# Moving 45 on-chip buffers to other addresses: attention into a SoLU feed-forward layer on one core

## The chip, the core and the metric

The program runs on one core of a Trainium2 chip. The metric is the device time of one execution in microseconds (us). A kernel is timed in several runs and its median is given; beside that, one further execution was profiled, and all durations of single instructions below come from that one. The engines are named as in the profile: PE (matmuls) and PEld (its weight loads), DVE, ACT and POOL (elementwise work), SP (the queue that issues all DMA transfers).

## What is computed

The reference is an attention between 512 tokens and 32 states in each of 8 batches and 8 heads, in both directions, and behind it a feed-forward layer with a softmax-weighted activation and a layer norm:

```python
# x: (8, 8, 512, 64), state: (8, 8, 32, 64), scale = 1 / 8
a = softmax(scale * x @ state.T)              # tokens read the states
xread = a @ state
a2 = softmax(scale * state @ x.T)             # states read the tokens
sread = a2 @ x
x = concat([xread, sread], axis=2)            # as rows: 8 * (512 + 32) = 4352 x 512

h = x @ w_in                                  # 4352 x 1024
sm = softmax(h)
solu = h * sm
mu, var = solu.mean(-1), solu.var(-1)
ln = (solu - mu) / sqrt(var + 1e-6) * g_ln
out = ln @ w_out                              # 4352 x 512
```

Inputs and output are float32.

## The kernel before, in words

**Tiling.** The 4352 rows are 34 tiles `t` of 128: 32 tiles hold the token rows (four for each batch), and the last two hold the state rows of all batches. A tile goes through five steps. `H`: PE multiplies into `h`, a 128x1024 PSUM tile (line 472). `C`: DVE takes the row maximum (479), ACT the exponential `e` (482), DVE the product `u` (485), ACT or DVE subtracts the mean in place (490, 492), ACT squares and sums (497), and POOL makes the row factor (499 to 502). `D`: DVE transposes 32x32 blocks into `ub` (509), a DMA writes it to a DRAM buffer (326), and another reads it back as `back` with the blocks in their final places (331). `T`: `back` is split into a rounded part `uh` (ACT or DVE, 141 and 143) and the rest `ul` (POOL or DVE, 146). `O`: PE multiplies them with the split weights `wohi` and `wolo` (546), ACT or DVE scales the result into `osb` (553, 555), and a DMA writes that out (559). In a matmul here the 128x128 piece of `uh` or `ul` is loaded as weights, and 512 columns of `wohi` or `wolo` stream past it.

**Before the tiles** the weights are loaded as `raw`, turned into float32 (`wf`) and split; for each batch the states are multiplied with `w_in` (`swf`, `vt`), the scores are made and go through both softmaxes (`e2`, `a`, `aT`, `ath`, `atl`).

**What sets the order.** Each engine's instructions stand in the order of a fixed list, `ORDER`, and nothing is rescheduled. Each step is a generator, and each token of the list runs one step to its next `yield`.

**What sets the addresses.** SBUF tiles come from pools, and a pool lays its tiles down one behind the other in the order of their first use. There are 45 common blocks of 4096 bytes in each partition. Which block a tile takes is fixed too: the string `PLACES["k4"]` has one character for each tile in order of use, and each character is one of the 45 places, so that a block holds one tile after the other. Before the change the blocks come from the pool `work`, the same one that gives the small tiles: `r` (2048 bytes), `s2` (2048), `sc` (16), `m1` and `z1` (up to 128 each), `sm` (32), `sr` (512) and `osb` (2048). A small tile that is first used between two blocks therefore stands between them and pushes the later blocks on. The pool `const`, laid down first in both kernels, ends at byte 21216, which is 5 x 4096 + 736.

Added up, the 45 blocks begin at these positions (start address modulo 4096):

| position before | blocks | pushed there by |
|---|---|---|
| 736 | 1 (place 0, at 21216) | nothing; it is the first |
| 2784 | 22 | three `r` tiles (6144 bytes), further on also the two `s2` tiles (4096) |
| 2848 | 2 | the two `sc` tiles (32 each) |
| 2976 | 15 | `m1` (128) |
| 3104 | 5 | `z1` (128) |

Place 0 holds, one after the other, `raw0`, `vt7_0`, `ub8`, `u10`, `uh10`, `atl4`, `a7`, `ub28` and `ub31` (the number is that of the weight piece, the batch or the tile). The eight operands that stream in the `O` step stay at one place each from the splitting of the weights on: three of the four `wohi` blocks begin at 2976 and one at 2784; three of the four `wolo` blocks begin at 2784 and one at 3104.

Of the kernel before, what the change touches and what calls it, by code (L numbers as in the profile page):

```python
# [8 lines left out]
F32 = mybir.dt.float32  # L9
# [7 lines left out]
B, H, S, NS, D = 8, 8, 512, 32, 64  # L17
DM, DF = 512, 1024
P = 128
NP = H // 2  # L20
NT = S // P
NJ = H * NS // P
# [61 lines left out]
    k4='0123456789ABCDEFGHIJKLMNOPQRSTUVWXYZabcdefghi0148BAFEKLQPNTOefcdMR6USgJVcTdLNOaZgI6APCWY7BDcKXbLhgiG'  # L84
# [20 lines left out]
def attention_then_solu_ffn(ctx, tc, xT, xn, stB, w_in, w_out, g, out):  # L105
    nc = tc.nc
    const = ctx.enter_context(tc.tile_pool(name="const", bufs=1))
    work = ctx.enter_context(tc.tile_pool(name="work", bufs=1))
    dram = ctx.enter_context(tc.tile_pool(name="dram", bufs=B + NTILES, space=bass.MemoryType.DRAM))
    kept = ctx.enter_context(tc.tile_pool(name="kept", bufs=4, space=bass.MemoryType.DRAM))  # L110
# [7 lines left out]
    def place(tag):  # L118
        return f"{tag}_{next(places[tag])}"

    def sbuf(tag, shape, dtype, name):
        if tag in places:
            return work.tile(shape, dtype, tag=place(tag), name=name, bufs=1)
        return work.tile(shape, dtype, tag=tag, name=name, bufs=SLOTS[tag])

    def block(shape, dtype, name):
        return sbuf("k4", [P, *shape], dtype, name)

    def bank(shape, name):
        return ps_t.tile([P, *shape], F32, tag=place("t"), name=name, bufs=1)  # L130
# [41 lines left out]
    def load_st(k):  # L172

        st[k] = block([2 * NP * 2, 2, NS], F32, f"st{k}")
        nc.sync.dma_start(st[k].rearrange("p (k c s) h n -> p k c s (h n)", k=2, c=NP), stB[:, k:k + 2])
        yield
# [24 lines left out]
    def load_x(b, j):  # L201
        x_of[b, j] = block([2, S], F32, f"xT{b}_{j}")
        nc.sync.dma_start(x_of[b, j], xT[b][:, 2 * j:2 * j + 2])
        yield

    def load_xn(b, i):

        xn_of[b, i] = block([2, H * D], F32, f"xn{b}_{i}")
        nc.sync.dma_start(xn_of[b, i], xn[b].rearrange("(c f) p h -> (f p) c h", c=4)[:, 2 * i:2 * i + 2])
        yield  # L210
# [113 lines left out]
    def to_dram(x, name):  # L324
        d = dram.tile([P * DF], F32, tag="d", name=name)
        nc.sync.dma_start(d.rearrange("(p f) -> p f", p=P), x)
        return d

    def from_dram(out, d):

        nc.sync.dma_start(out.rearrange("p (q c) -> p q c", q=4), d.rearrange("(q p c) -> p q c", q=4, p=P))
# [10 lines left out]
    def softmax_tokens(b):  # L342

        sc = sbuf("sc", [P, 4], F32, f"sc{b}")
        for j in range(NJ):
            ps = scores[b][j]
            nm, z = sc[:, j:j + 1], sc[:, 2 + j:3 + j]
            nc.vector.tensor_reduce(nm, ps, AX.X, ALU.max, negate=True)
            yield
            nc.gpsimd.tensor_scalar_mul(nm, nm, float(D) ** -0.5)  # L350
            yield
            if j == 0:
                e2 = block([NJ, S], F32, f"e2T{b}")
            nc.scalar.activation(e2[:, j, :], ps, AF.Exp, bias=nm, scale=float(D) ** -0.5, accum_out=z)
            yield
        z = zs[b] = sc[:, 2:4]
        nc.vector.tensor_scalar_add(z, z, 1e-9)
        nc.vector.reciprocal(z, z)
        yield
        blocks = block([NJ * S], F32, f"e2b{b}")  # L360

        nc.vector.transpose(blocks.rearrange("x (p j c) -> x j p c", p=4, j=NJ),
                            e2.rearrange("x j (p c) -> x j p c", p=4))
        yield
        d = to_dram(blocks, f"e2d{b}")
        yield
        e2s[b] = block([NJ * S], F32, f"e2_{b}")
        from_dram(e2s[b], d)
        yield
# [219 lines left out]
    for b in range(B):  # L589
        for i in range(2):  # L590
            step(f"LT{b}{i}", load_x, b, i)
            step(f"Ln{b}{i}", load_xn, b, i)
            step(f"V{b}{i}", state_w_in, b, i)
        step(f"S{b}", score, b)
        step(f"E{b}", softmax_tokens, b)
        if b in OPT["ah"]:
            for part in range(2):
                step(f"Ah{b}{part}", softmax_states, b, part, 2)
        else:
            step(f"A{b}", softmax_states, b)  # L600
        step(f"R{b}", read_tokens, b)
        for j in range(NJ):
            step(f"Y{b}{j}", keep_state_w_in, b, j)
            step(f"Z{b}{j}", load_state_w_in, b, j)
            step(f"P{b}{j}", split_state_w_in, b, j)
# [49 lines left out]
```

## Time and profile before

| what | us |
|---|---|
| median of 3 runs | 372.08 |
| lowest and highest of them | 370.94, 375.21 |
| the profiled execution | 372.63 |
| its span, from the first instruction to the last | 370.8 |
| its mean granted TensorE clock | 0.978 |

The profile is read as follows. A group row gives line, engine, operation, the tiles written and read, the sizes and the count, then the busy time in us, the mean of one in ns, and the idle time of the engine ahead of these instructions with what ended it. A tile row gives for all instructions that touch a tile the least, the median and the greatest duration in ns. The chain of waits follows the work that ended last back from the end, and gives shares of the span. Buffer numbers are left out of names (`ub` stands for all 34 of them), so a single tile is found by its time.

### The profile page before, as it was taken

To read this page: it belongs to the slowest core of one execution; us is meant where nothing else is said; L and a number is where in the kernel's file an instruction comes from. 1 tells how busy PE (TensorE), PEld (TensorE's weight loads), DVE (VectorE), ACT (ScalarE), POOL (GpSimd) and SP (SyncE) were. 2 spreads that over 40 slices of the span, in tenths; PEclk is the share of its full clock that TensorE was granted. 3 is DMA by queue.
4 is the path that set the end of the run, shared out by engine and by line. 5 is a ranking of instruction groups with operands and counts; after the bars stand their busy time and mean duration, and the time that the engine had idled before them with its cause. 6 is when DMAs were issued, how large, how long until landed. Compare 5 with 4: busy or idle time off the path is not lost.

```text
span 370.8 us, 6200 instructions
## 1 busy us (share of the span) xinstructions
PE 348.9 (94%) x2274; PEld 255.3 (69%) x2274; DVE 282.4 (76%) x393; ACT 216.3 (58%) x350; POOL 190.5 (51%) x245
## 2 busy tenths in 40 slices
PE   5498999989999999999999999999999999999990
PEld 4163334468777877778877777887888887888890
DVE  4679999979897978969979998969579577665400
ACT  3277998876768863847755656372474645424230
POOL 2131365565678662527776247376866616702540
PEclk9599999999999999999999999999999999999996
DMA  7996999999879999486895796846662454245412
GB/s 254 396 401 226 348 307 337 345 351 319 315 241 324 343 354 319 166 277 203 266 358 203 244 369 232 276 158 248 217 229 95 151 189 170 85 177 183 150 63 56
DMA packets 47051, 92.16 MB, mean 249 GB/s; under 512 B 4141, under 2 KB 25901, under 8 KB 47021
## 3 DMA queue, kind: packets, MB, share of 16 engines
q1 hardware_dynamic: 47020, 91.77, 70.7%
q8 instruction: 18, 0.29, 0.3%
q14 instruction: 13, 0.10, 0.1%
HBM read 54.53 MB, written 37.22 MB: 247 GB/s over the span
## 4 chain that ended last, share of the span: by engine, by line
PE 70%; DMA 13%; DVE 9%; ACT 3%; issue 2%; SPq 1%; POOL 1%; DVEq 0%; POOLq 0%
PE o L546 40%; PE h L472 22%; DMA ut<-ub 4%; DMA back<-ut 3%; DMA st<-stB_dram 3%; PE swps L198 2%; DMA xT<-xT_dram 2%; PE sps L198 2%; PE srps L420 2%; PE swph L198 2%; DVE ub L509 1%; DMA e<-e2d 1%; DVE sm L479 1%; DVE u L485 1%; ACT u L490 1%
## 5 line engine op out<-in xcount | busy, mean ns | idle before, releaser
L146 POOL TENSOR_TENSOR ul<-back,uh 128x512 fp32r<-128x512 f32 x46 | 61.2, 1335 | 49.5 <-DVE uh L143 23.8
L546 PE MATMUL o<-wolo,uh 128*128 128x512 f32 (+1 forms) x264 | 72.2, 388 | 0.0
L546 PE MATMUL o<-wohi,ul 128*128 128x512 f32 (+1 forms) x264 | 72.2, 387 | 0.0
L546 PE MATMUL o<-wohi,uh 128*128 128x512 f32 (+1 forms) x264 | 71.5, 389 | 0.4 <-ACT uh L141 0.2
L482 ACT ACTIVATE e<-h,sm 128x1024 f32<-128x1024 f32 x34 | 37.8, 1113 | 40.0 <-DVE sm L479 36.7
L546 PEld LDWEIGHTS o<-wohi,uh 128*128 128x128 f32 x264 | 48.3, 188 | 12.9 <-ACT uh L141 0.9
L485 DVE SCALAR_TENSOR_TENSOR u<-h,e 128x1024 f32<-128x1024 f32 x34 | 41.4, 1217 | 20.6 <-ACT e L482 20.2
L546 PEld LDWEIGHTS o<-wohi,ul 128*128 128x128 f32 x264 | 48.7, 188 | 11.6 <-issue 0.8
L546 PEld LDWEIGHTS o<-wolo,uh 128*128 128x128 f32 x264 | 48.3, 188 | 12.2 <-issue 1.7
L479 DVE TENSOR_REDUCE sm<-h 128x1 f32<-128x1024 f32 x34 | 41.3, 1213 | 15.4 <-PE h L472 8.4
L509 DVE STREAM_TRANSPOSE ub<-u 128x1024 f32<-128x1024 f32 x34 | 42.0, 1237 | 5.2 <-ACT u L490 4.6
L141 ACT ACTIVATE uh<-back 128x512 fp32r<-128x512 f32 (+1 forms) x46 | 28.2, 624 | 26.3 <-DMA back<-ut 26.3
L497 ACT ACTIVATE e<-u 128x1024 f32<-128x1024 f32 x34 | 35.8, 1053 | 5.6 <-DVE u L492 5.3
L553 ACT ACTIVATE osb<-o,sm 128x512 f32<-128x512 f32 (+1 forms) x29 | 19.3, 668 | 27.8 <-PE o L546 9.7
L472 PE MATMUL h<-swh,ath 128*128 128x512 f32 x112 | 35.3, 401 | 0.0
L472 PE MATMUL h<-swl,ath 128*128 128x512 f32 x112 | 35.0, 394 | 0.0
L472 PE MATMUL h<-swh,atl 128*128 128x512 f32 x112 | 34.9, 394 | 0.0
L490 ACT ACTIVATE u<-u,sm 128x1024 f32<-128x1024 f32 x20 | 23.0, 1150 | 14.4 <-DVE u L485 14.4
L146 POOL TENSOR_TENSOR swl<-swf,swh 128x1024 fp32r<-128x1024 f32 x11 | 26.6, 2418 | 3.3 <-ACT swh L141 2.1
L248 POOL TENSOR_TENSOR wf<-wf,r 128x512 uint32<-128x512 uint32 x9 | 11.8, 1311 | 27.7 <-DVE wf L245 11.3
L472 PEld LDWEIGHTS h<-swh,ath 128*128 128x128 f32 x112 | 20.6, 188 | 6.2 <-issue 1.2
L472 PEld LDWEIGHTS h<-swh,atl 128*128 128x128 f32 x112 | 21.0, 188 | 4.9
(87 smaller groups left out, 531.6 us busy)
## 6 DMA issues: line engine op xcount, KB each, us to landing
ut<-ub SPq DMA_DIRECT2D x34, 512.0 KB, 3.5
back<-ut SPq DMA_DIRECT2D x34, 512.0 KB, 4.6
out_dram<-osb SPq DMA_DIRECT2D x33, 256.0 KB, 3.5
xT<-xT_dram SPq DMA_DIRECT2D x16, 512.0 KB, 6.9
xn<-xn_dram SPq DMA_DIRECT2D x16, 512.0 KB, 5.7
kept<-vt SPq DMA_DIRECT2D x12, 512.0 KB, 6.3
swf<-kept SPq DMA_DIRECT2D x12, 512.0 KB, 5.7
raw<-w_in_dram SPq DMA_DIRECT2D x8, 512.0 KB, 8.8
```

Source lines behind the costliest of these rows:

```text
L141: nc.scalar.activation(out, src, AF.Copy)
L146: engine(k).tensor_tensor(out=out, in0=a, in1=hi.bitcast(F32), op=ALU.subtract)
L198: nc.tensor.matmul(banks[j][at:at + NS, :], state_of(b, head), moving(head // 2)[h * D:(h + 1) * D], start=True, stop=True)
L472: nc.tensor.matmul(ph[t][:, cols], left[l][:, p, tok], weights[:, cols], start=(p, l, r) == (0, 0, 0), stop=(p, l, r) == (parts - 1, *kind ...
L479: nc.vector.tensor_reduce(nm, ph[t], AX.X, ALU.max, negate=True)
L482: nc.scalar.activation(e, ph[t], AF.Exp, bias=nm, accum_out=z)
L485: nc.vector.scalar_tensor_tensor(out=u, in0=ph[t], scalar=1.0, in1=e, op0=ALU.mult, op1=ALU.mult, accum_out=su)
L490: nc.scalar.activation(u, u, AF.Identity, bias=su, scale=-float(DF))
L497: nc.scalar.activation(e, u, AF.Square, scale=float(DF) ** -0.5, accum_out=ss)
L509: nc.vector.transpose(ub, us[t][0])
L546: nc.tensor.matmul(po, ut[t][l][:, f, :], w[NP + f // 2][:, f % 2, cols], start=(hf, l, w is wohi, q) == (0, 0, True, 0), stop=(hf, l, q) ...
L553: nc.scalar.activation(o[:, cols], po, AF.Copy, scale=us[t][1])
```

## The change

The 45 blocks get a pool of their own, `blocks`, which is opened between `const` and `work`. Only one helper, `block()`, gives out tiles of this kind; it now asks that pool, with the same tag for each place. A local variable that had the pool's new name is renamed.

```diff
@@ attention_then_solu_ffn
     const = ctx.enter_context(tc.tile_pool(name="const", bufs=1))
+    blocks = ctx.enter_context(tc.tile_pool(name="blocks", bufs=1))
     work = ctx.enter_context(tc.tile_pool(name="work", bufs=1))
...
     def block(shape, dtype, name):
-        return sbuf("k4", [P, *shape], dtype, name)
+        return blocks.tile([P, *shape], dtype, tag=place("k4"), name=name, bufs=1)
...
-        blocks = block([NJ * S], F32, f"e2b{b}")
-
-        nc.vector.transpose(blocks.rearrange("x (p j c) -> x j p c", p=4, j=NJ),
+        turned = block([NJ * S], F32, f"e2b{b}")
+
+        nc.vector.transpose(turned.rearrange("x (p j c) -> x j p c", p=4, j=NJ),
                             e2.rearrange("x j (p c) -> x j p c", p=4))
         yield
-        d = to_dram(blocks, f"e2d{b}")
+        d = to_dram(turned, f"e2d{b}")
```

The blocks now stand one behind the other from byte 21216 on, and as each is 4096 bytes long, all 45 begin at position 736 modulo 4096. Place 0 stays where it was; the 22 blocks at 2784 move by 2048 bytes modulo 4096, the others by 2112, 2240 and 2368. The small tiles come behind the blocks, from byte 205536 on. 45 times 4096 is a whole multiple of 4096, so each small tile keeps the position modulo 4096 that it had (`r` at 736, 2784 and 736, `s2` at 2784 and 736, `osb` at 3744 and 1696), and `sm`, `sr` and `osb`, which were last in the pool before too, even keep their addresses.

On each engine and in SP's queue the same instructions stand in the same order, with the same sizes and the same semaphore waits. Which tile shares a block with which is the same too. Only addresses differ.

## The prediction

> **What bounds the kernel now.** I read the page's first part and the chain of waits first, to see which engine the end hangs on, and then busy time by stage. The first row gives busy time and share of the span for each engine, the next two the chain's shares by engine and by line, the table the same stretch by stretch.
>
> ```profile
> span 370.8 us, 6200 instructions
> PE 348.9 (94%) x2274; PEld 255.3 (69%) x2274; DVE 282.4 (76%) x393; ACT 216.3 (58%) x350; POOL 190.5 (51%) x245
> ...
> PE 70%; DMA 13%; DVE 9%; ACT 3%; issue 2%; SPq 1%; POOL 1%; DVEq 0%; POOLq 0%
> PE o L546 40%; PE h L472 22%; DMA ut<-ub 4%; DMA back<-ut 3%; DMA st<-stB_dram 3%; PE swps L198 2%; DMA xT<-xT_dram 2%; PE sps L198 2%; PE srps L420 2%; PE swph L198 2%; DVE ub L509 1%; DMA e<-e2d 1%; DVE sm L479 1%; DVE u L485 1%; ACT u L490 1%
> ```
>
> ```profile
> core 0: us, PE busy (x) PEld busy (x) DVE busy (x) ACT busy (x) POOL busy (x), PEclk, DMA share, GB/s
> 0.00:80.00 80.00, 68.07 (x522) 33.55 (x522) 64.81 (x104) 55.74 (x95) 30.70 (x44) 0.94 0.91 326
> 80.00:180.00 100.00, 99.33 (x659) 76.25 (x660) 85.77 (x112) 67.92 (x108) 62.17 (x75) 1.00 0.83 287
> 180.00:280.00 100.00, 99.17 (x711) 77.96 (x710) 83.73 (x115) 59.16 (x94) 60.55 (x76) 1.00 0.73 255
> 280.00:345.00 65.00, 65.00 (x289) 52.52 (x288) 44.99 (x59) 27.84 (x46) 28.11 (x37) 1.00 0.43 150
> 345.00:371.00 26.00, 17.38 (x99) 14.99 (x97) 3.08 (x6) 5.61 (x10) 8.97 (x16) 0.88 0.25 82
> ```
>
> From 80 to 345 us PE is busy in 263.5 of 265 us. The time there is the number of matmuls times the pace of one. Before 80 us transfers take part (DMA share 0.91), and behind 345 us the last tile's chain runs out. So a new address can reach the end in three ways: by PE's pace, by transfers (13% of the chain, 48.2 us), or by DVE, ACT and POOL where the chain passes through them (9%, 3% and 1%).
>
> **The change, part by part.** It adds no instruction, removes none and moves none; no wait is new, and no DMA passes another. The only cost it can have is a duration that depends on where a tile begins. The trace of before already holds tiles at five positions, and place 0 stands at 736, where all blocks go. So I look for that dependence in it, engine by engine.
>
> PE first, as it carries 70% of the chain. The chain's longest unbroken stretches give the pace; its columns are the start, the length in us, and the piece of work with its number of matmuls. Then the group rows by form for streamed operands, and the spread of the weight loads in the tile view.
>
> ```profile
> 168.56 9.25 PE o L546 x40
> ...
> 280.73 9.73 PE o L546 x42
> ...
> 312.79 8.78 PE o L546 x38
> ```
>
> ```profile
> L546 PE MATMUL o<-wolo,uh 128*128 128x512 f32 x248 | 69.9, 395 | 0.0
> L546 PE MATMUL o<-wohi,ul 128*128 128x512 f32 x248 | 69.8, 394 | 0.0
> L546 PE MATMUL o<-wohi,uh 128*128 128x512 f32 x248 | 69.1, 396 | 0.4 <-ACT uh L141 0.2
> ```
>
> ```profile
> L546 PEld LDWEIGHTS o<-wohi,uh x264: 186/188/192, 81.6 to 361.0; 128*128 128x128 f32 x132
> L546 PEld LDWEIGHTS o<-wolo,uh x264: 186/188/192, 82.4 to 361.5; 128*128 128x128 f32 x132
> L546 PEld LDWEIGHTS o<-wohi,ul x264: 186/188/192, 83.3 to 362.0; 128*128 128x128 f32 x132
> ```
>
> The pace is 9250/40 = 231.3, 9730/42 = 231.7 and 8780/38 = 231.1 ns. `wohi` streams mostly from 2976, `wolo` mostly from 2784 (three of four blocks each), and their means are 394 to 396 ns: 1 ns between the kinds, and no more between the two rows of `wohi` itself. The weights `uh` and `ul` come from all five positions, and 264 loads lie within 186 to 192 ns. I take 0 for PE. The bound is 1 ns on each 512-column matmul of this kind. Those are 3 x 248 here, 3 x 112 in `H` and 3 x 16 for the state rows (the rows of `h` read the same way), 1128 in all: 1.1 us either way.
>
> DVE, ACT and POOL next. The first two rows cover all 34 tiles at every position (least/median/greatest ns). The timeline rows behind them (start and duration in us) are instructions on place 0, already at 736: `u10` written at 131.99 and read at 137.40, changed in place at 133.42, `ub28` written at 301.58, and `atl4` written at 177.37.
>
> ```profile
> L485 DVE SCALAR_TENSOR_TENSOR u<-h,e x34: 1164/1224/1227, 44.3 to 343.1; 128x1024 f32<-128x1024 f32 x34
> ...
> L509 DVE STREAM_TRANSPOSE ub<-u x34: 1186/1245/1247, 46.7 to 345.2; 128x1024 f32<-128x1024 f32 x34
> ...
> L490 ACT ACTIVATE u<-u,sm x20: 1133/1152/1156, 45.6 to 306.5; 128x1024 f32<-128x1024 f32 x20
> ```
>
> ```profile
> 131.99 1.23 DVE L485 SCALAR_TENSOR_TENSOR u<-h,e 128x1024 f32<-128x1024 f32 x1 [1.27 <-ACT e L482]
> ...
> 137.40 1.24 DVE L509 STREAM_TRANSPOSE ub<-u 128x1024 f32<-128x1024 f32 x1
> ```
>
> ```profile
> 133.42 1.14 ACT L490 ACTIVATE u<-u,sm 128x1024 f32<-128x1024 f32 x1
> ```
>
> ```profile
> 301.58 1.25 DVE L509 STREAM_TRANSPOSE ub<-u 128x1024 f32<-128x1024 f32 x1
> ```
>
> ```profile
> 177.37 2.41 POOL L146 TENSOR_TENSOR atl<-aT,ath 128x1024 fp32r<-128x1024 f32 x1
> ```
>
> ```profile
> L146 POOL TENSOR_TENSOR atl<-aT,ath 128x1024 fp32r<-128x1024 f32 x4 | 9.7, 2426 | 6.4 <-ACT ath L141 5.4 <-DVE ath L143 1.0
> ```
>
> At the new position each takes its group's median to 0.01 us (1.23 against 1.224, 1.24 and 1.25 against 1.245, 1.14 against 1.152, 2.41 against a mean of 2.426). I take 0. The bound is 0.01 of about 1.2 us, some 0.8%, on the 13% of the chain that lies on these engines (48.2 us): 0.4 us either way. Elsewhere PE's work covers it; PE's own operands would come late only if that cover of POOL and DVE ran out.
>
> Transfers are last, and the least sure, because their time to landing depends above all on what else is in flight. The tile view of `ub` gives over all (least/median/greatest):
>
> ```profile
> DMA to landing us min/median/max: 2.6/3.5/6.6
> ```
>
> I compare single transfers at quiet moments: at 302.9 us (`ub28`, from place 0 at 736), at 259.5 (`ub23`, from 2976) and at 154.4 (`ub11`, from 2784). The three answers, one for each moment, follow in that order.
>
> ```profile
> L326 SPq DMA_DIRECT2D ut<-ub x1: 319/319/319, 302.9 to 302.9; - x1
> ...
> DMA to landing us min/median/max: 2.6/2.6/2.6
> ```
>
> ```profile
> L326 SPq DMA_DIRECT2D ut<-ub x1: 332/332/332, 259.5 to 259.5; - x1
> ...
> DMA to landing us min/median/max: 2.6/2.6/2.6
> ```
>
> ```profile
> L326 SPq DMA_DIRECT2D ut<-ub x1: 319/319/319, 154.4 to 154.4; - x1
> ...
> DMA to landing us min/median/max: 2.6/2.6/2.6
> ```
>
> All three land after 2.6 us. I take 0; the row's last digit leaves 0.05 in 2.6, or 2%, and on the 48.2 us of the chain that is 1.0 us either way.
>
> [...] The quiet transfers from 736, 2784 and 2976 show no difference in their tenth of a us; none from 2848 or 3104 was as quiet.
>
> The sum: 372.63 us of the profiled execution (370.8 span, 1.8 around it) plus 0, between 2.5 less and 2.5 more if all bounds fell on one side. That execution lies 0.55 above the median of the three runs, so against the median the forecast is 372.08 plus 0, rounded to 372.0.
>
> **The rivals.** First, slower: every tile now begins at the same position, and each long transfer's row crosses a multiple of 4096 after 3360 bytes, where before it was 992 to 1312 for all but place 0. If transfers between blocks and DRAM took longer for it, the place to feel it is the bounce `ut<-ub`, `back<-ut` in the chain and the loads before 80 us, where DMA is busy 91% of the time. At 10% more the chain's 48.2 us give 4.8 us, 376.9 in all; it decides from 7.7% on (3.7 of 48.2). For it speaks only that one transfer in three of these is not seen at a quiet moment; against it, that `ub28` with the new crossing landed in 2.6 us like the others, and that every row crosses one such multiple before as well as after.
>
> Second, faster: PE streams more smoothly when its operands begin elsewhere. For 1%, 3.7 us, each of the 1128 matmuls would have to gain 3.3 ns of 231; the stretches above differ by 0.6 and the kinds by 1 to 2. At 4 ns it would give 367.6. Against it stands also that `wolo` mostly keeps its lower address bits (2784 to 736 is 2048 exactly).
>
> Third, the change does something else than it says, a wait or another sharing of blocks that came with the second pool. The waits and the sharing are the same in both programs, so this would have to come from the chip's side, and I give it no time of its own.
>
> **How the numbers follow.** A change of 1% is about what a measurement of this kernel can tell from none; its three runs lie 1.1% apart. No dependence on position: 0.83, at 372.0. The transfers' rival: 0.09. PE's rival: 0.08. The range takes the 2.5 us of bounds on each side of 372.0 and, as the before's own runs reach 3.1 above their median, a little more above: 369.4 to 375.4. Faster by over 1%: 0.08; within 1%: 0.83; slower by over 1%: 0.09.
>
> **What would show it.** Right: the group means of `o`, `h`, `u`, `ub` and `ul` within 1% of those above, PE busy 263 to 264 us in 80 to 345, chain stretches of 231 to 232 ns a matmul, `ut<-ub` and `back<-ut` with least landings of 2.6 and about their medians of before. Wrong: an `o` or `h` pace off by more than 3 ns; a least landing of `ut<-ub` over 2.8; or two-operand work on POOL or DVE with a new median, since all its operands now begin alike. A difference of the time without any of these would be the runs' own spread.

## The result, and the profile after

The changed kernel takes 369.57 us (median of 14 runs, 367.19 to 371.0), the kernel before 372.25 (14 runs, 370.94 to 375.21) beside it. The ratio is 0.992, with a 95% interval of 0.9896 to 0.9944: a gain of 0.8%, small, but a ratio of 1 lies outside the interval. The forecast was 372.0. The profiled execution took 370.28 us, 2.35 less than that of before; its span fell by 2.5.

The page's first part and its chain come first, then the three middle rows of the table by stretch, with the same columns as before. All lines of the kernel's body are one further down now (`o` is L547, `h` L473).

```profile
span 368.3 us, 6200 instructions
PE 345.5 (94%) x2274; PEld 255.2 (69%) x2274; DVE 282.3 (77%) x393; ACT 216.4 (59%) x350; POOL 190.0 (52%) x245
...
PE 59%; DMA 17%; DVE 13%; ACT 4%; issue 2%; SPq 1%; POOL 1%; DVEq 0%; POOLq 0%; ACTq 0%
```

```profile
80.00:180.00 100.00, 98.24 (x661) 76.42 (x646) 85.39 (x112) 67.04 (x106) 62.01 (x74) 1.00 0.84 287
180.00:280.00 100.00, 98.44 (x713) 78.26 (x712) 84.36 (x116) 59.83 (x95) 61.03 (x77) 1.00 0.74 255
280.00:345.00 65.00, 65.00 (x293) 53.47 (x293) 46.39 (x61) 28.86 (x47) 27.49 (x37) 1.00 0.43 150
```

PE's busy time fell by 3.4 us. DVE, ACT and POOL stand where they stood, within 0.5. But from 80 to 345 us PE is busy in less of the time than before: 98.24 + 98.44 + 65.00 = 261.68 of 265 against 263.50. It waits 3.3 us there where it waited 1.5.

The two longest stretches of PE in the chain, and the six groups of fp32r matmuls with 512 columns, answer to those shown before:

```profile
279.75 9.52 PE o L547 x42
...
311.27 8.61 PE o L547 x38
```

```profile
L547 PE MATMUL o<-wolo,uh 128*128 128x512 f32 x248 | 69.0, 391 | 0.0
L547 PE MATMUL o<-wohi,ul 128*128 128x512 f32 x248 | 68.8, 390 | 0.0
L547 PE MATMUL o<-wohi,uh 128*128 128x512 f32 x248 | 68.3, 393 | 2.4 <-ACT uh L142 2.1 <-DVE uh L144 0.3
L473 PE MATMUL h<-swh,ath 128*128 128x512 f32 x112 | 34.9, 397 | 0.2
L473 PE MATMUL h<-swl,ath 128*128 128x512 f32 x112 | 34.6, 391 | 0.0
L473 PE MATMUL h<-swh,atl 128*128 128x512 f32 x112 | 34.4, 389 | 0.0
```

A matmul now takes 9520/42 = 226.7 ns and 8610/38 = 226.6, where the same stretches of before gave 231.7 and 231.1. Every group's mean is 3 to 5 ns shorter. The busy times of the three `o` groups fell from 208.8 to 206.1 us and those of the three `h` groups from 105.2 to 103.9, so 4.0 us in all. The span fell by 2.5. The difference is in the waits of PE (engine and line, what it waited for; us in total, times, longest), where before only one of 0.2 stood for `uh`:

```profile
PE o L547 <- ACT uh L142: 2.1, 3, 1.4
```

The longest of these, 1.4 us, stands at `o` of tile 6. The first rows below are the chain there in the kernel before, the next ones the chain of the changed kernel from 104 us on, and the last two are rows of SP's queue in the changed kernel's timeline:

```profile
107.29 6.60 DMA back<-ut
...
114.60 2.59 PE o L546 x10
```

```profile
103.67 2.69 DMA ut<-ub
...
106.37 7.83 DMA back<-ut
...
114.90 2.56 PE o L547 x10
```

```profile
104.56 0.73 SPq L309 DMA_DIRECT2D swf<-kept  x1
105.34 0.63 SPq L304 DMA_DIRECT2D kept<-vt  x1
```

PE is done with the work ahead of tile 6 some 0.9 us earlier than before (at 113.5 us, the start 114.90 less the wait of 1.4, against 114.4), but the tile's data come no earlier: `back6` is issued 0.92 us earlier and lands 0.31 us later, at 114.20 against 113.89. It lands 7.83 us after its issue, the longest of all `back` tiles (median 4.6), behind those two transfers, put in the queue just ahead of it. They stood there before too, where `back6` took 6.60 us. So with the order of work as it stands, part of what PE gains at 227 ns a matmul is given back in waits.

The other two terms of the forecast, in the tile views of `u` and of `ub` (least/median/greatest, in ns for instructions, in us for the landing):

```profile
L486 DVE SCALAR_TENSOR_TENSOR u<-h,e x34: 1161/1224/1227, 44.2 to 341.1; 128x1024 f32<-128x1024 f32 x34
...
L510 DVE STREAM_TRANSPOSE ub<-u x34: 1185/1245/1252, 46.6 to 343.1; 128x1024 f32<-128x1024 f32 x34
```

```profile
DMA to landing us min/median/max: 2.6/3.4/7.2
```

The medians 1224 and 1245 ns are those of before to the nanosecond (so is ACT's, 1152), and `ut<-ub` lands after 2.6 at least and 3.4 at the median (3.5 before). No difference by position showed there.

### The profile page after: what moved, and what is told of

The parts are those of the page before. It is cut to its first block, busy times and chain, and to the rows that moved or that the text cites. A ratio compares the mean times of both kernels' runs of the same rounds, so it can differ in the third digit from the quotient of the medians.

```text
span 368.3 us, 6200 instructions
## 1 busy us (share of the span) xinstructions
PE 345.5 (94%) x2274; PEld 255.2 (69%) x2274; DVE 282.3 (77%) x393; ACT 216.4 (59%) x350; POOL 190.0 (52%) x245
## 4 chain that ended last, share of the span: by engine, by line
PE 59%; DMA 17%; DVE 13%; ACT 4%; issue 2%; SPq 1%; POOL 1%; DVEq 0%; POOLq 0%; ACTq 0%
PE o L547 33%; PE h L473 18%; DMA ut<-ub 6%; DMA back<-ut 6%; DMA st<-stB_dram 3%; PE swps L199 2%; DVE ub L510 2%; PE sps L199 2%; DMA xT<-xT_dram 2%; PE swph L199 2%; DVE u L486 2%; DVE sm L480 2%; DMA e<-e2d 1%; PE srps L421 1%; ACT e L483 1%
## 5 line engine op out<-in xcount | busy, mean ns | idle before, releaser
L147 POOL TENSOR_TENSOR ul<-back,uh 128x512 fp32r<-128x512 f32 x46 | 61.1, 1334 | 47.5 <-DVE uh L144 22.5
L547 PE MATMUL o<-wohi,uh 128*128 128x512 f32 (+1 forms) x264 | 70.7, 386 | 2.4 <-ACT uh L142 2.1
L547 PE MATMUL o<-wolo,uh 128*128 128x512 f32 (+1 forms) x264 | 71.4, 385 | 0.0
L547 PE MATMUL o<-wohi,ul 128*128 128x512 f32 (+1 forms) x264 | 71.1, 383 | 0.0
L547 PEld LDWEIGHTS o<-wohi,uh 128*128 128x128 f32 x264 | 48.2, 188 | 14.4 <-ACT uh L142 3.4
L547 PEld LDWEIGHTS o<-wohi,ul 128*128 128x128 f32 x264 | 48.7, 188 | 10.7 <-issue 0.8
L547 PEld LDWEIGHTS o<-wolo,uh 128*128 128x128 f32 x264 | 48.3, 188 | 11.3 <-issue 1.7
L473 PE MATMUL h<-swh,ath 128*128 128x512 f32 x112 | 34.9, 397 | 0.2
L473 PE MATMUL h<-swl,ath 128*128 128x512 f32 x112 | 34.6, 391 | 0.0
L473 PE MATMUL h<-swh,atl 128*128 128x512 f32 x112 | 34.4, 389 | 0.0
L473 PEld LDWEIGHTS h<-swh,ath 128*128 128x128 f32 x112 | 20.6, 188 | 6.1 <-issue 1.3
L473 PEld LDWEIGHTS h<-swh,atl 128*128 128x128 f32 x112 | 21.0, 188 | 4.5
```

Of the source, the lines that this page charges most:

```text
L147: engine(k).tensor_tensor(out=out, in0=a, in1=hi.bitcast(F32), op=ALU.subtract)
L473: nc.tensor.matmul(ph[t][:, cols], left[l][:, p, tok], weights[:, cols], start=(p, l, r) == (0, 0, 0), stop=(p, l, r) == (parts - 1, *kind ...
L547: nc.tensor.matmul(po, ut[t][l][:, f, :], w[NP + f // 2][:, f % 2, cols], start=(hf, l, w is wohi, q) == (0, 0, True, 0), stop=(hf, l, q) ...
```

## The experiments

Three theories stood against each other for PE's pace. A: it counts whether the two operands of a matmul, the loaded weights and the streamed columns, begin alike modulo some number of bytes. Before, the blocks stood at 224, 32 and 160 modulo 256, in mixed pairs; now all stand at 224. B: PE is held up by the SBUF traffic of the other engines and DMAs, and the new addresses take that away. C: position 736 itself is a good one, whatever the other operand does.

**e1 and e2: PE by itself, and with the other engines at work.** A small kernel writes two wide fp32r tiles `mv` and `w` and runs stretches of 96 matmuls of the kernel's form. Only start addresses differ between stretches. The attention and the feed-forward layer are left out, and the output is a constant.

```diff
+ for name, shifts in SEGMENTS.items():
+     for k in range(96):
+         m, l = shifts(k)                         # bytes added to each start
+         m = (k % 4 * 2048 + m) // 4
+         l = (k // 8 % 4 * 4096 + k % 8 * 512 + l) // 4
+         nc.tensor.matmul(ps, w[:, l:l + P], mv[:, m:m + 512], start=k == 0, stop=k == 95)
+         if k % 5 == 0:                           # e2 only
+             nc.vector.tensor_tensor(out=db, in0=da, in1=src, op=ALU.mult)
+             nc.scalar.activation(ab, aa, AF.Copy)
+             if k % 10 == 0:
+                 nc.gpsimd.tensor_tensor(out=pb, in0=pa, in1=src, op=ALU.mult)
```

> Only PE works, in thirteen stretches of 96 matmuls that differ in where the streamed operand and the weights begin; attention and feed-forward are left out and the output holds a constant. Theory A (PE's own two operands set its pace: when their start addresses differ modulo 512 from matmul to matmul, each costs some 4 ns more): stretches 'same' and 'again' at 226 to 227 ns a matmul, 'walt', 'malt', 'both' and 'asbefore' at 230 to 232. Theory B (other engines that read and write at other positions disturb PE): all thirteen stretches at 226 to 227 ns. If a constant difference is enough, 'wplusq' to 'wplusd' tell it: 226 to 227 if only a change of the difference costs, 230 to 232 if the difference itself does.

> The same thirteen stretches with DVE, ACT and POOL working beside PE on tiles at 736 and 2784 (the same computation is left out). Theory A: the same table as PE alone. Theory B: 'same' rises above 227 here and not in the run with PE alone, and no stretch differs much from another.

The chain of e1 (start, length in us, stretch). In `wplusq`, `wplush`, `wplust` and `wplusd` the weights begin 64, 128, 192 and 256 bytes on; in `walt` they alternate between 0 and 192 every four matmuls; `asbefore` repeats 96 pairs of positions from the kernel before; in `again` nothing is shifted.

```profile
35.93 22.68 PE wplusq L80 x96
...
59.38 22.58 PE wplush L80 x96
...
82.72 22.29 PE wplust L80 x96
...
105.78 22.07 PE wplusd L80 x96
...
175.20 22.36 PE walt L80 x96
...
267.58 22.49 PE asbefore L80 x96
...
290.84 22.06 PE again L80 x96
```

Against `again`, a shift of 64 costs (22.68 - 22.06)/96 = 6.5 ns a matmul, 128 costs 5.4, 192 costs 2.4, and 256 nothing (0.1). The pairs of the kernel before cost 4.5 ns, close to what it lost there: the starts of its matmuls of this kind lie 231.4 ns apart on the mean in the trace (1092 of them, with 150 to 250 ns to the next start), those of the changed kernel, counted likewise, 227.3. PE was alone in e1: no other engine was busy in these stretches, and the DMA share in them was 0.00. The groups of e2 by form come next (count, busy us, mean ns), and the row by stretch that covers `same` (columns as in the table above):

```profile
L80 PE MATMUL asbefore<-mv,w 128*128 128x512 f32 x96 | 22.5, 394 | 0.8 <-DVE o L86 0.8
...
L80 PE MATMUL same<-mv,w 128*128 128x512 f32 x96 | 22.1, 390 | 0.0
L80 PE MATMUL again<-mv,w 128*128 128x512 f32 x96 | 22.1, 390 | 0.8 <-DVE o L86 0.8
```

```profile
0.00:30.00 30.00, 27.24 (x149) 24.20 (x150) 27.86 (x12) 28.96 (x29) 27.59 (x15) 1.00 0.00 1
```

In e1 these three groups have the means 394, 390 and 390 as well. Not all three engines worked beside each of them, though: DVE, ACT and POOL were all busy in `same`, but ACT had done its share at 274 us and POOL at 392, so `asbefore` and `again`, behind 498 us, had DVE alone beside them. The four stretches behind `same`, `wplusq` to `wplusd`, ran with all three. They began after PE had waited 28 to 35 us for DVE, and the granted clock was lower (0.81 from 61 to 100 us, around `wplusq`; 0.780 over the whole of e2, 0.965 over e1), so their group means (427 ns for `wplusq`, 397 in e1) can't be set beside those of e1; but from the 17th matmul on their starts lie 233.3, 233.4, 228.9 and 226.8 ns apart on the mean, where e1 has 233.3, 232.3, 228.9 and 226.7. So B falls for the engines. It falls for transfers too as far as these runs go: e1 has the whole effect without any, and the changed kernel keeps 226.7 ns from 280 to 345 us with a DMA share of 0.43.

`walt` tells one thing more: half its pairs are alike and half differ by 192, and it costs 3.1 ns, more than either kind by itself (0 and 2.4). A mixture is not the mean of its parts: from the 17th matmul on, the alike pairs in it take 229.5 ns from start to start, those in `again` 226.7.

**e3: another position, the same for all.** The blocks begin at 0 modulo 4096.

```diff
-    mhalf = const.tile([P, 1], F32, name="mhalf")
+    mhalf = const.tile([P, 848], F32, name="mhalf")[:, :1]
```

> All 45 blocks at position 0 modulo 4096 instead of 736. Theory A (the operands begin alike): time as in the changed kernel, 369.6 us within 1, o and h at 226 to 227 ns a matmul. Theory C (736 is a good place, or the old ones were bad places by themselves): the pace and the time change, to 372 us or to below 368.

369.66 us over 10 runs, ratio 0.9928 (0.9895 to 0.9962), and the chain has the same stretches:

```profile
279.79 9.52 PE o L547 x42
...
311.28 8.61 PE o L547 x38
```

226.7 and 226.6 ns again. C falls: 736 is no better than 0.

**e4: a pool of their own, but two positions.** The changed kernel with 192 bytes between the blocks, so that the first part of them begins at 736 and the rest at 928.

```diff
+    laid = []
     def block(shape, dtype, name):
-        return blocks.tile([P, *shape], dtype, tag=place("k4"), name=name, bufs=1)
+        tag = place("k4")
+        if tag == "k4_M" and not laid:
+            laid.append(blocks.tile([P, 48], F32, tag="gap", name="gap", bufs=1))
+        return blocks.tile([P, *shape], dtype, tag=tag, name=name, bufs=1)
```

> The changed kernel with 192 bytes laid between the 22nd and the 24th block or so, so that half of the blocks stand at 736 and half at 928, as 2784 and 2976 stood to each other before. Theory A: the slow pace comes back, 230 to 232 ns a matmul and 372 us within 1. Theory C: one of the positions is the old good one and the other one is 736 plus 192, so the pace lies between, 228 to 230 ns.

371.31 us over 10 runs, ratio 0.9987 (0.9962 to 1.0011): the gain is gone. The chain's stretches:

```profile
279.34 9.74 PE o L552 x42
...
311.42 8.82 PE o L552 x38
```

That is 231.9 and 232.1 ns. The pool, the order and the sharing are the changed kernel's; only the pairs are mixed again.

**e5 and e9: the kernel before, with its small tiles widened.** No pool of its own; the three small tiles that stood between the blocks take 256 bytes each, so that all blocks begin at 224 modulo 256 (at 736, 2784, 3296, 3552 and 3808 modulo 4096).

```diff
-        sc = sbuf("sc", [P, 4], F32, f"sc{b}")
+        sc = sbuf("sc", [P, 64], F32, f"sc{b}")[:, :4]
...
-        m = sbuf("m1", shape, F32, f"m1_{b}_{part}")
+        m = sbuf("m1", [P, 64, 1], F32, f"m1_{b}_{part}")[:, :shape[1]]
...
-        z = sbuf("z1", shape, F32, f"z1_{b}_{part}")
+        z = sbuf("z1", [P, 64, 1], F32, f"z1_{b}_{part}")[:, :shape[1]]
```

> The kernel before, with its one pool and its order of first use, but sc, m1 and z1 widened to 256 bytes each, so that the 45 blocks stand at 736, 2784, 3296, 3552 and 3808: five positions modulo 4096, all 224 modulo 256. Theory A in the form that the difference of PE's two operands modulo 256 decides: 226 to 228 ns a matmul and 369.6 us within 1. If the operands must begin alike modulo 4096, or the own pool matters: 231 ns and 372 us within 1.

> The kernel of e5_small_tiles_padded again (before, with its three small tiles widened to 256 bytes so that all block positions agree modulo 256), for a profile, since that of e5 was one of 1943.89 us. Theory A (what counts is whether the two operands of a matmul begin alike modulo 256 bytes): groups of o and h at 390 to 393 ns, a start each 226 to 228 ns, span near 368 us. If the pool of its own mattered by anything else than these positions: 394 to 396 ns and a start each 231 ns.

e5 took 369.74 us, ratio 0.9948 (0.9916 to 0.9979). Its profiled execution alone took 1943.89 us, with `o` groups of about 1700 ns a matmul; nothing in the kernel accounts for that, and its cause stays open. e9 is the same kernel in one further execution: 369.87 us, span 367.9, with `o` groups of 390 to 393 ns and this chain:

```profile
279.33 9.52 PE o L546 x42
...
310.77 8.61 PE o L546 x38
```

So the gain comes without the pool. Agreement modulo 256 was enough here, with five positions modulo 4096: 226.7 and 226.6 ns a matmul.

**e6: all pairs alike, and unlike.** The changed kernel with the eight blocks of `wohi` and `wolo` 192 bytes further on, so that every `o` matmul has the same difference: its weights begin 64 bytes ahead modulo 256, which was the dearest in e1. The `h` matmuls keep their agreement.

```diff
+    streamed = ctx.enter_context(tc.tile_pool(name="streamed", bufs=1))
...
+        if tag[-1] in "SPbLhGAM":
+            if not laid:
+                laid.append(streamed.tile([P, 48], F32, tag="gap", name="gap", bufs=1))
+            return streamed.tile([P, *shape], dtype, tag=tag, name=name, bufs=1)
```

> The changed kernel with the eight blocks of wohi and wolo 192 bytes further on, all other blocks at 736. In the o matmuls the weights then begin 64 modulo 256 above the streamed operand, always; the h matmuls keep a difference of 0. Theory A with the prices of PE alone: o at 233 ns, h at 227, and 744 x 6.6 = 4.9 us more PE work than in the changed kernel, so 372 to 374 us, as slow as before or slower. If only a change of the difference from one matmul to the next costs: o at 227 and 369.6 us.

373.07 us over 10 runs, ratio 1.0022 (0.9992 to 1.0051). The chain and two groups:

```profile
281.62 9.80 PE o L555 x42
...
313.77 8.87 PE o L555 x38
```

```profile
L555 PE MATMUL o<-wolo,uh 128*128 128x512 f32 x248 | 70.3, 396 | 0.0
...
L481 PE MATMUL h<-swh,atl 128*128 128x512 f32 x112 | 34.6, 391 | 0.0
```

233.3 and 233.4 ns in `o`: 6.6 above the pace with agreeing starts, as 64 bytes cost in e1 (6.5). One layout of the same program gives 226.7, another 233.3.

**e8: which differences.** e1's kernel, the weights shifted by 16 (`wa`), 32, 48, 64, 96, 160, 192 (`wg`), 224 (`wh`) and 240 bytes (`wi`), the streamed operand by 64 (`mq`) and 192 (`mt`), and both by 64 (`bothq`).

```diff
-    wplusq=lambda k: (0, 64),
+    wa=lambda k: (0, 16),
...
+    wi=lambda k: (0, 240),
+    mq=lambda k: (64, 0),
+    mt=lambda k: (192, 0),
+    bothq=lambda k: (64, 64),
```

> Only PE works, thirteen stretches of 96 matmuls, the weights 0, 16, 32, 48, 64, 96, 160, 192, 224 and 240 bytes further on than the streamed operand (same, wa to wi), the streamed operand 64 and 192 further on (mq, mt), and both 64 (bothq); the computation is left out. Theory A: 'same' and 'bothq' at 226.7 ns, 'wd' and 'wg' at 233.3 and 228.9 as measured, 'mq' as 'wg' and 'mt' as 'wd' if the difference modulo 256 is all that counts; the others lie above 226.7. If reads are counted in pieces of 64 bytes, 'wa' to 'wc' stay at 226.7.

The chain of e8:

```profile
34.53 22.67 PE wa L80 x96
...
175.27 22.28 PE wg L80 x96
198.32 22.68 PE wh L80 x96
221.77 22.07 PE wi L80 x96
244.61 22.27 PE mq L80 x96
267.64 22.67 PE mt L80 x96
291.08 22.11 PE bothq L80 x96
```

`bothq` is as fast as no shift at all, `mq` costs what weights 192 on cost (22.27 and 22.28) and `mt` what weights 64 on cost (22.67). So in these stretches the time went by the difference of the two starts, modulo 256: fast at 0 (22.11, `bothq`) and at 240 (22.07), between at 192 (22.28), slow at 16 already (22.67) and at 224 (22.68). The other case on record, in which 16 to 48 stay fast, falls: `wa`, `wb` and `wc` took 22.67 us each.

**e7, e10, e11 and e12: what is given back.** If the new waits of PE come from `back` tiles that land late, then putting other transfers behind them should win it back. In e7 the load of `swf3` and the store of `vt7` (the two rows ahead of `back6` above) are issued behind `back6`; every tile keeps its block. In e10 the store of `ut24` is also issued ahead of the load of a tile for batch 6.

```diff
-... A3*2 A2 E2 Z30 E2 Y70 T5 O4 T5 O4
-P21*2 H7*2 C7 H8*2 O5 D6 O5 O4 E2 E3 ...
+... A3*2 A2 E2*2 T5 O4 T5 O4
+P21*2 H7*2 C7 H8*2 O5 D6 Z30 Y70 O5 O4 E2 E3 ...
...
-H26 C22 O22 E6 R6*2 C25 R7 C24 R7 R6*2 D25 H27*3 D24 A7 D24 O21 T24 O24*2
+H26 C22 O22 D24 E6 R6*2 C25 R7 C24 R7 R6*2 D25 H27*3 A7 D24 O21 T24 O24*2
```

> The changed kernel with two transfers (the load of swf for batch 3, the store of vt for batch 7) issued behind the load of back for tile 6 instead of ahead of it. If part of PE's gain is given back where PE waits for that tile: the wait of 1.8 us ahead of its first o matmul, at 113 us, shrinks to under 0.8 and the time falls by 0.5 to 1 us, to about 368.8. If the wait has another cause, it stays and the time is 369.6 within 0.5.

> e7_two_transfers_later, with the store of ut24 issued ahead of the load of a tile that batch 6 needs only later, so that back24 lands earlier. If what the faster PE gives back is the wait for the back tiles, the gap ahead of o of tile 24 (0.75 us) falls to about 0.3 and the time is 367.8 to 368.3 us. If that gap is set by something else on that queue or by the transfer itself, the time stays at e7's 368.3.

> The changed kernel again, beside the next one on the same chip: 369 to 370.5 us, a ratio to before of 0.990 to 0.995, and the gap ahead of o of tile 6 at 1.0 to 1.8 us.

> The kernel of e7_two_transfers_later again, to see whether it is faster than the changed kernel. If the wait ahead of o of tile 6 lies on the path that sets the end, its median is 0.8 to 1.8 us under that of e11_changed_again; if later waits take back what is gained there (as in e10_third_transfer), the two lie within 0.5 us of each other.

e7: 368.28 us over 6 runs, ratio 0.9908 (0.9872 to 0.9945). A row of its table by stretch, and its only wait for `uh`:

```profile
80.00:180.00 100.00, 100.00 (x665) 78.67 (x657) 87.82 (x116) 69.32 (x110) 64.45 (x75) 1.00 0.84 292
```

```profile
PE o L544 <- ACT uh L139: 0.4, 1, 0.4
```

PE has no gap left from 80 to 180 us, where the changed kernel had 1.76 us of them. e10 brought nothing further: 370.1 us over 9 runs (366.6 to 370.56), ratio 0.9917 (0.9885 to 0.9949), where 368.3 or less had been expected. Its wait ahead of tile 24 went, but in its profile others stand at tiles 20 (0.6 us), 15 (0.5) and 4 (0.5):

```profile
PE o L544 <- POOL ul L144: 0.6, 1, 0.6
PE o L544 <- DVE uh L141: 0.5, 1, 0.5
...
PE o L544 <- ACT uh L139: 0.5, 1, 0.5
```

Side by side, the changed kernel took 370.23 us (e11, 11 runs, without a twelfth of 374.3; ratio 0.9938, 0.9914 to 0.9961) and that of e7 368.63 (e12, 6 runs from 367.93 to 372.38; 0.9902, 0.9866 to 0.9937). e11's profile has the gap ahead of tile 6 again (a wait of 1.2 us for `uh`). e12's profiled execution, at 372.38 us the longest of its six, has none there, but one of 3.5 us at tile 15, whose `back` tile landed 6.20 us after its issue (the wait, and the row of the chain):

```profile
PE o L544 <- DVE uh L141: 3.5, 1, 3.5
```

```profile
198.31 6.20 DMA back<-ut
```

So the move takes the wait at tile 6 away in all three profiles with it (e7, e10, e12). The medians of the kernel of e7 are 1.3 us better than the changed kernel's at another time (368.28 against 369.57) and 1.6 side by side (368.63 against 370.23); the intervals of the ratios overlap, so what the move is worth in time is not settled. Which `back` tile comes late changes from one execution to the next, and part of the gain is lost there.

## Why the prediction was wrong

**"I take 0 for PE" was the step that failed,** with its bound of 1.1 us. PE's term came to 4.0 us less in the groups of `o` and `h`, 3.6 ns on each of the 744 `o` matmuls (2.7 us) and 3.9 on each of the 336 of `h` (1.3 us).

The reason given, that kinds of operands at different positions differ by 1 ns, compared the wrong things. It looked at where each operand stands; what told in the runs is how far apart the two starts of one matmul are, modulo 256 (226.7 ns at 0 in the changed kernel, 233.3 at 64 in e6). Each of the groups compared was a mixture of such differences, and so each had about the same slow mean: e4 shows that mixture again with two positions only, and `walt` that alike pairs in a mixture don't keep the pace they have by themselves. Even sorted by difference, the starts in the trace of before give 230.8 ns for the 387 alike pairs and 232.2 for the 310 that differ by 64, 1.4 apart, where e1 and e6 give over 6. Nothing in that trace held the fast case in a long row: at most ten alike pairs follow each other there. In e4, where rows reach 18, the first two of a row take 230.8 ns on the mean and those from the eleventh on 227.2 (18 matmuls, so few). That was the point to see: five positions in the trace of before didn't cover the new layout, in which all operands agree. For DVE and the transfers place 0 was a sample of what came; for PE a block at 736 was none, since it was paired with others.

The 186 to 192 ns of the weight loads said nothing either; in the fast stretch `same` of e1 they last as long (187/188/192). The price shows in the matmuls' pace (22.68 us for the 96 of `wplusq`, 22.06 for those of `again`).

**PE's rival had the right direction and nearly the right size**: 4 ns a matmul, "367.6". Its mechanism was named too loosely ("begin elsewhere"): in e3 and e9 the blocks stand elsewhere and agree, and both give 226.7 and 226.6 ns; in e4 they don't agree, and it gives 231.9 and 232.1. The remark against it, that `wolo` keeps its lower address bits, was no argument, since its partner's bits moved. It overshot by 2 us because it priced PE alone: of 4.0 us, 1.8 came back as waits between 80 and 345 us (3.3 against 1.5). 4.0 less 1.8 is 2.2 of the span's 2.5; the rest is in the stretches ahead of 80 and behind 345 us, where transfers also take part (a DMA share of 0.91 ahead of 80 us and of 0.25 behind 345, before and after), and wasn't followed further. These are figures of one profiled execution each; e11's has 3.8 us of waits there.

**That the time came out inside the stated range, 369.4 to 375.4, and within 1% of before, was luck.** The range was made of small bounds on each side of 0. PE's 4.0 us alone would have ended below it, at 368.1. The waits, which the prediction does not have, took the time back into it; without the wait at tile 6, e7's 368.28 lies below it again.

**DVE, ACT and POOL at 0 were right** (DVE's and ACT's medians equal to the ns, POOL's mean of `ul` 1334 ns after 1335), **and so were the transfers** (`ut<-ub` lands after 2.6 us at least as before, and its median went from 3.5 to 3.4; nothing of the rival's 10%).

**The list of signs worked**: "an `o` or `h` pace off by more than 3 ns" was what came. The third rival falls, since e9 has the gain without a second pool and e4 has the pool without the gain.

DVE, ACT and POOL did not slow PE where all three worked beside it: e2 has `same` at 390 ns and `wplusq` at 233.3 from start to start, as e1 has. By nothing but the starts of its operands, 96 matmuls took 22.06 us (`again` of e1) to 22.77 (`we` of e8, the weights 96 bytes on). Why this is so no run shows; 240 being fast (22.07) and 224 slow (22.68) fits no simple rule that was tried here. Also open is which load counts: the next matmul's weights are loaded while one streams (from 58 to 90 us of e1 PE is busy 30.43 of 32 us and PEld 24.14), and in stretches with one difference the matmul's own weights and the next one's stand alike to the streamed columns.

## What to carry to other kernels

Where PE sets the time with fp32r matmuls that each load new weights, try the two operands of every matmul at starts that agree modulo 256 bytes: here that took a matmul from 231.4 ns to 227.3, so the small tiles between the large ones in the pool had cost 2% on each of these matmuls. When asking whether a layout matters, look at pairs of operands and at a long row of one pair, not at group means over mixtures, and measure it with a small kernel. The faster PE came sooner to what it waits for, and 1.8 of its 4.0 us went into waits: price the waits behind it, and look at what stands in the queue ahead of the transfer that ends them.

## What had not been expected of the hardware

- A 128x128x512 fp32r matmul goes by in 226.7 ns or in 233.3, by the difference of two start addresses alone (e6 against the changed kernel), and one of 16 bytes is enough ((22.67 - 22.07)/96 = 6.3 ns between `wa` and `wi` in e8).
- The pace of a pair went with the pairs around it: alternating between a difference of 0 and one of 192 (22.36 us, `walt` of e1) is slower than 192 throughout (22.29) and than 0 throughout (22.06).
- The float32 matmuls of the same kernel, not fp32r, did not change: `h<-swf,aT` has a mean of 609 ns before and after, though its blocks moved as well.
